# Loads of v for the first three chunks issued from GpSimd, and the first two scalings of k on VectorE, in a gated linear attention with a feed-forward layer behind it

## The chip, the core and the metric

The kernel runs on one core of a Trainium2 chip. The core has TensorE (matrix multiply, called PE in the profile, with its weight loads shown as PEld), VectorE (DVE), ScalarE (ACT), GpSimd (POOL) and SyncE (SP), which here does nothing but issue loads. The metric is the device time of one execution in microseconds (us); less is better. The kernel before has a median of 192.18 us over 11 runs.

## The reference

For each of 4 batches and 8 heads a state of 48 x 48 numbers is carried over 768 steps: it is decayed by alpha, row by row, and the outer product of k and v is added; the output is q times the state. The outputs of all heads are put side by side into rows of 384, and a feed-forward layer with a cosine gate follows:

```python
for t in range(S):
    state = alpha[:, :, t, :, None] * state + np.einsum('bhd,bhe->bhde', k[:, :, t], v[:, :, t])
    y[:, :, t] = np.einsum('bhd,bhde->bhe', q[:, :, t], state)
...
h = x @ w_in            # 3072 x 384 by 384 x 2048
g = h * np.cos(h)
return (g @ w_out).astype(np.float32)
```

## The kernel before

The 768 steps of a batch are cut into chunks of 128, so there are 24 chunks, each with all 8 heads: a tile has 128 rows (steps) and 8 x 48 columns. For a chunk the decay is turned into running sums of logarithms (ScalarE's logarithm in line 144, then a matmul with a triangle of ones in lines 157 and 161), and ScalarE takes the exponential of these and of their negatives (lines 177 and 175). k is multiplied by the one (`khat`, line 185) and q by the other (`qhat`, line 191), v is turned into bfloat16 (`vcast`, line 195), and a small tile `Em` holds the decay over the chunk (`emask`, line 200). TensorE transposes the scaled k and q (line 218), VectorE moves them out (line 224), TensorE forms the scores of each head (line 235), VectorE masks them (line 244), and TensorE forms the output from the scores and v (line 292) and from q and the state (line 289). The state is updated from k and v (line 260, then lines 272 and 274). The output is moved out (line 299), transposed (line 313) and moved out again (line 318), and goes through the feed-forward layer in two halves: matmul (line 330), cosine on ScalarE (line 338), gate on VectorE (line 344), matmul (line 352), eviction and store (lines 357 and 358).

Loads are of 192 KB. A chunk of k, q, v or alpha lies in memory as 8 heads of 128 rows of 48 floats, so each partition of the tile gets 8 runs of 192 bytes. `load` (lines 102 to 105) and `load_a` (line 100) issue them from SP, into pools of 6 tiles for each of k, q and v. The weights are four loads each of 768 KB (lines 111 and 124), cast by lines 115 and 117.

Nothing is scheduled by a planner. A string, `ORDER`, lists the steps by letter and chunk, and each engine does its share of them in that order; so each engine, and SP's queue of loads, works through a fixed list, and an instruction that waits holds up all that is behind it on its engine. `a0` loads alpha of chunk 0, `k0`, `q0`, `v0` the other inputs; `i0` is the logarithm of one chunk and `l1` that of chunks 2 and 3 together, `c0` and `C1` are the sums on TensorE, `d0` and `E1` the exponentials; `K0` is `khat`, `Q0` is `qhat`, `b0` is `vcast`, `E_0` is `emask`; `T0` are the transposes and `t0` their eviction, `A0` the scores, `m0` their masking, `Y0` the outputs, `y0` their eviction, `D0` the transposes of the output, `S0` and `u0` the state. `w19` are 19 matmuls on a tile of zeros (line 368), whose result is not used; there are 63 of these, all in the first part of the list. In what follows K0 and the like stand for these steps.

Before the first step of `ORDER`, VectorE clears some tiles and GpSimd builds two triangles of ones and an identity matrix. Of the scaling steps, Q0 and Q1 are on VectorE (`eng = nc.vector if j < 2 else nc.gpsimd` in `qhat`); all of K, all of b and all of E_ are on GpSimd.

Of the kernel before, what the change touches and what calls it, by code (L numbers as in the profile page):

```python
# [12 lines left out]
ALU = mybir.AluOpType  # L13
# [3 lines left out]
def kernel(  # L17
# [10 lines left out]
    nc = tc.nc  # L28
    B, H, S, D = q.shape
# [41 lines left out]
    khb, qhb = kqb[:, :, 0], kqb[:, :, 1]  # L71
# [16 lines left out]
    w2 = consts.tile([C, NF, DM], BF, tag="w2")  # L88

    a_t, q_t, k_t, v_t, cp_t, icp_t = {}, {}, {}, {}, {}, {}  # L90

    def rows(t, j):
        b, c = j // NC, j % NC
        return t[b, :, c * C : (c + 1) * C, :].rearrange("h s d -> s h d")
# [6 lines left out]

    def load(nm, src, d, j):
        t = inpool.tile([C, H, D], FP, tag=nm)
        nc.sync.dma_start(out=t, in_=rows(src, j))
        d[j] = t

    QF = DF // 4
# [74 lines left out]

    def khat(j):
        icp = icp_t[j // 2][:, j % 2]
        nc.gpsimd.tensor_tensor(out=khb[:, j % 3, :, 0:D], in0=k_t.pop(j),  # L185
                                in1=icp.rearrange("s (h d) -> s h d", h=H), op=ALU.mult)

    def qhat(j):
        cp = cp_t[j // 2][:, j % 2]
# [172 lines left out]
    def warmup(n):  # L362
# [8 lines left out]
    dve, act_e = nc.vector, nc.scalar  # L371
    units = {
        "a": load_a, "k": lambda j: load("k_sb", k, k_t, j), "q": lambda j: load("q_sb", q, q_t, j),
        "v": lambda j: load("v_sb", v, v_t, j), "z": load_w1, "Z": load_w2,
        "r": lambda h: cast_w1(h, dve, 0, 2), "s": lambda h: cast_w1(h, act_e, 2, 3), "R": cast_w2,

        "i": lambda j: ln(j, 1), "c": lambda j: cums(j, 1), "d": lambda j: exps(j, 1),
        "l": lambda g: ln(2 * g, 2), "C": lambda g: cums(2 * g, 2), "E": lambda g: exps(2 * g, 2),
        "K": khat, "Q": qhat, "b": vcast, "E_": emask,
        "T": transposes, "t": ev_transposes, "S": state, "u": ev_state,  # L380
        "A": scores, "m": mask_scores, "Y": outputs, "y": ev_outputs, "D": x_transposes, "B": ev_x,
# [4 lines left out]
    }  # L386

    ORDER = (
        "a0 i0 q0 c0 v0 a1 k0 k1 d0 Q0 E_0 i1 v1 K0 w19 T0 q1 t0 a2 b0 c1 d1 Q1 k2 v2 w2 A0 a3 K1 w3 T1 m0 t1 "
        "w6 A1 m1 a4 a5 Y0 b1 E_1 l1 y0 w7 D0 k3 B0 b2 q2 C1 E1 K2 q3 S0 u0 w3 Y1 Q2 Q3 y1 E_2 q4 w3 S1 u1 w3 "  # L390
        "D1 B1 w2 T2 t2 w4 A2 m2 l2 C2 w2 Y2 y2 K3 E2 k4 K4 w3 D2 B2 a6 a7 Q4 l3 w2 T3 t3 C3 w1 S2 u2 A3 m3 "
        "E3 v3 b3 w2 T4 t4 E_3 E_4 w5 A4 S3 z0 r0 s0 z1 z2 z3 r1 s1 F0 f_0 u3 m4 Y3 s2 F1 f_1 r2 y3 E_6 Z1 D3 "
# [23 lines left out]
    for u in ORDER.split():  # L416
        nm = u.rstrip("0123456789")
# [29 lines left out]
```

## Time and profile before

| | us |
|---|---|
| median of 11 runs | 192.18 |
| lowest and highest run | 191.54, 193.23 |
| the profiled execution's own time | 192.28 |
| its span in the profile | 190.5 |
| TensorE busy | 181.5 (95% of the span) |
| VectorE, ScalarE, GpSimd busy | 128.3, 119.1, 74.8 |

The span runs from the first to the last instruction that the profile records; 1.78 us of the execution's own time lie around it. Where the profile names what ended an idle time, it goes by the semaphore that came last. Instructions that only issue a transfer are not counted as busy time of an engine; the timeline shows them under SPq and ACTq, with the time that the issuing takes, and the landing is told apart from it: the 24 loads of v are issued from SP, with a median of 4.5 us from issue to landing. Of the bytes, 29.14 MB went over SP's queue and 4.72 MB over ScalarE's, which stores the output; there is no queue of GpSimd's among them. In the first 40th of the span (4.76 us) TensorE's row shows 0, in the others 9, up to the last with 2.

### The profile page before, as it was taken

The page shows a single profiled execution, that of the slowest core. Times are in us where ns is not written, and L with a number is a line of the kernel's source. Part 1 is how long each engine was busy: PE and PEld are TensorE (multiplying, and loading weights), DVE is VectorE, ACT ScalarE, POOL GpSimd, SP SyncE. Part 2 cuts the span into 40 slices and gives each one's busy share as a digit, 9 for nine tenths or more (in the row PEclk, how much of TensorE's full clock was granted, in tenths as well). Part 3 has the DMA queues.
Part 4 walks back from the last instruction along what each step waited for, and adds up shares of the span by engine and source line. Part 5 has one row for each costly group of instructions (what it writes and reads, how often), then busy time and mean ns, then how long its engine had stood idle before and what let it go on. Part 6 is the DMA issues. An engine that isn't in the chain of part 4 may idle for free.

```text
span 190.5 us, 5668 instructions
## 1 busy us (share of the span) xinstructions
PE 181.5 (95%) x2406; PEld 138.3 (73%) x2410; DVE 128.3 (67%) x159; ACT 119.1 (63%) x135; POOL 74.8 (39%) x116
## 2 busy tenths in 40 slices
PE   0999999999999999999999999999999999999992
PEld 0344545998766888697887688968769877797761
DVE  6128457999695489739667886895587685578520
ACT  3211447789555868985974989888596363364522
POOL 3422763212923451852971747155450475010000
PEclk9999999999999999999999999999999999999999
DMA  6999999999999999899999889997966899221112
GB/s 122 189 186 187 160 287 364 344 371 213 200 225 228 211 176 230 180 205 204 219 193 171 167 128 174 153 214 150 193 132 135 187 181 186 65 64 24 41 45 83
DMA packets 123225, 34.22 MB, mean 180 GB/s; under 512 B 116544, under 2 KB 121664, under 8 KB 123200
## 3 DMA queue, kind: packets, MB, share of 16 engines
q1 hardware_dynamic: 119744, 29.14, 82.1%
q10 hardware_dynamic: 3456, 4.72, 7.5%
q8 instruction: 19, 0.31, 0.7%
q14 instruction: 6, 0.05, 0.1%
HBM read 25.17 MB, written 4.72 MB: 157 GB/s over the span
## 4 chain that ended last, share of the span: by engine, by line
PE 88%; DMA 6%; POOL 2%; DVE 1%; ACT 1%; issue 1%; SPq 1%; DVEq 0%; ACTq 0%
PE t L330 33%; PE o_new L352 30%; PE w_new L368 8%; PE t L235 3%; PE t L218 3%; PE t L292 2%; DMA t<-kqb 2%; PE cum_new L157 2%; PE t L260 2%; PE t L289 2%; DMA t<-in_k_dram 2%; DMA a_new<-in_alpha_dram 2%; POOL kqb L185 2%; PE t L313 2%; PE cum_new L161 1%; DVE t L244 1%
## 5 line engine op out<-in xcount | busy, mean ns | idle before, releaser
L330 PE MATMUL t<-x,w 128*128 128x128 bf16 x1152 | 70.4, 219 | 0.0
L352 PE MATMUL o_new<-w,g_new 128*128 128x384 bf16 x384 | 68.8, 326 | 0.0
L344 DVE TENSOR_TENSOR g_new<-t,c_sb 128x1024 bf16<-128x1024 f32 x48 | 57.8, 1218 | 15.3 <-ACT c_sb L338 14.9
L330 PEld LDWEIGHTS <-w 128*128 128x128 bf16 x1152 | 65.6, 98 | 1.5
L338 ACT ACTIVATE c_sb<-t,halfpi 128x1024 bf16<-128x1024 f32 x48 | 52.3, 1112 | 18.5 <-PE t L330 15.6
L352 PEld LDWEIGHTS <-g_new 128*128 128x128 bf16 x384 | 35.4, 98 | 20.2
L244 DVE TENSOR_TENSOR t<-t,mask_f 128x1024 bf16<-128x1024 f32 x24 | 29.0, 1216 | 3.1 <-PE t L235 3.1
L185 POOL TENSOR_TENSOR kqb<-t,icp_new 128x384 bf16<-128x384 f32 x24 | 23.9, 1000 | 17.7 <-ACT icp_new L175 10.8
L274 POOL TENSOR_TENSOR ub<-sc,Em 128x384 bf16<-128x384 f32 x16 | 13.3, 829 | 39.6 <-DVE sc L272 39.6
L357 ACT ACTIVATE o_sb<-o_new 128x384 f32<-128x384 f32 x24 | 11.7, 488 | 26.0 <-PE o_new L352 26.0
L191 POOL TENSOR_TENSOR kqb<-t,cp_new 128x384 bf16<-128x384 f32 x22 | 22.0, 1008 | 12.0 <-DMA t<-in_q_dram 10.7
L299 DVE CAST t<-t 128x384 bf16<-128x384 f32 x24 | 13.3, 554 | 11.9 <-PE t L292 11.9
L175 ACT ACTIVATE icp_new<-cum_new 128x768 f32<-128x768 f32 (+1 forms) x13 | 9.8, 757 | 15.6 <-PE cum_new L161 15.1
L195 POOL CAST vpb<-t 128x384 bf16<-128x384 f32 x24 | 12.4, 518 | 18.1 <-DMA t<-in_v_dram 15.4
L368 PE MATMUL w_new<-warm 128*128 128x512 bf16 x63 | 19.0, 432 | 0.3 <-issue 0.2
L224 DVE COPY t<-t 128x1024 bf16<-128x1024 bf16 x13 | 8.9, 688 | 10.2 <-PE t L218 10.1
L144 ACT ACTIVATE lnab<-a_new 128x768 bf16<-128x768 f32 (+1 forms) x13 | 10.3, 794 | 5.4 <-DMA a_new<-in_alpha_dram 3.0
L137 ACT ACT_TABLE_LOAD x9 | 11.5, 1283 | 2.4 <-ACT o_sb L357 1.6
L338 ACT ACT_TABLE_LOAD x9 | 11.5, 1283 | 0.6 <-ACT o_sb L357 0.5
L272 DVE TENSOR_TENSOR sc<-t,ub 128x384 f32<-128x384 f32 x16 | 8.9, 554 | 4.5 <-PE t L260 4.4
L157 PE MATMUL cum_new<-lnab,triu_bf 128*128 128x384 bf16 x24 | 7.3, 333 | 4.5 <-ACT lnab L144 4.5
L292 PE MATMUL t<-vpb,t 128*128 128x48 bf16 x192 | 11.3, 183 | 0.2 <-DVE t L244 0.2
(43 smaller groups left out, 132.1 us busy)
## 6 DMA issues: line engine op xcount, KB each, us to landing
a_new<-in_alpha_dram SPq DMA_DIRECT2D x24, 192.0 KB, 4.6
t<-in_q_dram SPq DMA_DIRECT2D x24, 192.0 KB, 4.6
t<-in_v_dram SPq DMA_DIRECT2D x24, 192.0 KB, 4.5
t<-in_k_dram SPq DMA_DIRECT2D x24, 192.0 KB, 4.7
out_dram<-o_sb ACTq DMA_DIRECT2D x24, 192.0 KB, 3.3
w1f<-in_moe_w_in_dram SPq DMA_DIRECT2D x4, 768.0 KB, 7.5
w2f<-in_moe_w_out_dram SPq DMA_DIRECT2D x4, 768.0 KB, 10.9
t<-kqb SPq DMA_TRANSPOSE x11, 4.2
```

The lines of the kernel that those rows point to most:

```text
L185: nc.gpsimd.tensor_tensor(out=khb[:, j % 3, :, 0:D], in0=k_t.pop(j), in1=icp.rearrange("s (h d) -> s h d", h=H), op=ALU.mult)
L191: eng.tensor_tensor(out=qhb[:, j % 3, :, 0:D], in0=q_t.pop(j), in1=cp[:, 0:HD].rearrange("s (h d) -> s h d", h=H), op=ALU.mult)
L195: nc.gpsimd.tensor_copy(out=vpb[:, j % 3, :, 0:D], in_=v_t.pop(j))
L244: nc.vector.tensor_tensor(out=t.rearrange("s (h t) -> s h t", h=H), in0=A_ps.pop(j).rearrange("s (h t) -> s h t", h=H), in1=mask_f.unsquee ...
L274: eng.tensor_tensor(out=ub[:, us(j), :, 0:96].rearrange("r p (a e) -> r p a e", a=2), in0=sc.rearrange("r p (a e) -> r p a e", a=2), in1=E ...
L292: nc.tensor.matmul(t[:, h * D : (h + 1) * D], A_t[j][:, ACOL[h] * C : (ACOL[h] + 1) * C], vpb[:, j % 3, h], start=first, stop=True, skip_g ...
L299: nc.vector.tensor_copy(out=t, in_=y_ps.pop(j)[:, 0:HD])
L330: nc.tensor.matmul(t[:, f], w1[:, kk, ft * C : (ft + 1) * C], x_t[j][:, kk], start=(kk == 0), stop=(kk == 2))
L338: nc.scalar.activation(out=c_sb, in_=h_ps[j, half], func=AF.Sin, bias=halfpi, scale=1.0)
L344: nc.vector.tensor_tensor(out=g_new, in0=h_ps.pop((j, half)), in1=c_t.pop((j, half)), op=ALU.mult)
L352: nc.tensor.matmul(o_ps[j][:, 0:DM], g[:, f], w2[:, half * HF + f], start=(f == 0 and half == 0), stop=(f == HF - 1 and half == 1))
L368: nc.tensor.matmul(w_ps, warm[:, 0:C], warm, start=True, stop=True)
```

## The change

Three things are changed. The loads of v for chunks 0, 1 and 2 are issued by GpSimd instead of SP; a transfer issued from there has its descriptors made by software on GpSimd. In `ORDER` these three loads go to the front of the list, so that they are the first of its steps on GpSimd, behind the building of the constants; the loads left on SP keep their order. And K0 and K1 go from GpSimd to VectorE.

```diff
     def load(nm, src, d, j):
         t = inpool.tile([C, H, D], FP, tag=nm)
-        nc.sync.dma_start(out=t, in_=rows(src, j))
+        eng = nc.gpsimd if nm == "v_sb" and j < 3 else nc.sync
+        eng.dma_start(out=t, in_=rows(src, j))
         d[j] = t
...
     def khat(j):
         icp = icp_t[j // 2][:, j % 2]
-        nc.gpsimd.tensor_tensor(out=khb[:, j % 3, :, 0:D], in0=k_t.pop(j),
-                                in1=icp.rearrange("s (h d) -> s h d", h=H), op=ALU.mult)
+        eng = nc.vector if j < 2 else nc.gpsimd
+        eng.tensor_tensor(out=khb[:, j % 3, :, 0:D], in0=k_t.pop(j), in1=icp.rearrange("s (h d) -> s h d", h=H), op=ALU.mult)
...
     ORDER = (
-        "a0 i0 q0 c0 v0 a1 k0 k1 d0 Q0 E_0 i1 v1 K0 w19 T0 q1 t0 a2 b0 c1 d1 Q1 k2 v2 w2 A0 a3 K1 w3 T1 m0 t1 "
+        "v0 v1 v2 a0 i0 q0 c0 a1 k0 k1 d0 Q0 E_0 i1 K0 w19 T0 q1 t0 a2 b0 c1 d1 Q1 k2 w2 A0 a3 K1 w3 T1 m0 t1 "
         "w6 A1 m1 a4 a5 Y0 b1 E_1 l1 y0 w7 D0 k3 B0 b2 q2 C1 E1 K2 q3 S0 u0 w3 Y1 Q2 Q3 y1 E_2 q4 w3 S1 u1 w3 "
```

With this, VectorE's list begins, behind the clearing, with Q0, K0, t0, Q1, K1, m0, t1; GpSimd's, behind the constants, with the loads v0, v1, v2, then E_0, b0, b1, E_1, b2, K2; and SP's with the loads a0, q0, a1, k0, k1, q1, a2, k2, a3. Before, these were Q0, t0, Q1, m0, t1 on VectorE; E_0, K0, b0, K1, b1, E_1, b2, K2 on GpSimd; and a0, q0, v0, a1, k0, k1, v1, q1, a2, k2, v2, a3 on SP. TensorE's list is the same in both, all 63 matmuls on zeros included.

## Prediction

> **What bounds the kernel now.** I read the page's busy rows first, then TensorE's waits, then the timeline of the first 21 us, where the change lies.
>
> ```profile
> PE 181.5 (95%) x2406; PEld 138.3 (73%) x2410; DVE 128.3 (67%) x159; ACT 119.1 (63%) x135; POOL 74.8 (39%) x116
> ...
> DMA  6999999999999999899999889997966899221112
> ```
>
> TensorE is busy 181.5 of 190.5 us. Of the 9.0 us idle, 4.47 lie before its first matmul and 3.4 after its last (the final eviction starts at 187.14), so about 1.1 us is idle inside. The list of waits says the same; besides the first matmul's, no wait of TensorE is longer than 0.2 us:
>
> ```profile
> PE cum_new L157 <- ACT lnab L144: 4.5, 1, 4.5
> PE t L292 <- DVE t L244: 0.2, 1, 0.2
> PE t L218 <- POOL kqb L185: 0.2, 1, 0.2
> PE w_new L368 <- issue: 0.2, 1, 0.2
> ```
>
> So TensorE's own program, in its written order, sets the end. Part of it is filler: line 368's matmuls on a zero tile. The timeline (start, duration, engine, line, operation; in brackets the idle time before it and what ended that):
>
> ```profile
> 4.89 7.03 PE L368 MATMUL w_new<-warm 128*128 128x512 bf16 x19
> ...
> 6.02 0.57 POOL L200 TENSOR_TENSOR Em<-cp_new,m 128x8 f32<-128x8 f32 x1 [3.70 <-ACT cp_new L177]
> ...
> 6.99 0.52 ACT L144 ACTIVATE lnab<-a_new 128x384 bf16<-128x384 f32 x1 [1.05 <-DMA a_new<-in_alpha_dram]
> ...
> 8.07 0.99 POOL L185 TENSOR_TENSOR kqb<-t,icp_new 128x384 bf16<-128x384 f32 x1 [1.48 <-DMA t<-in_k_dram]
> ...
> 11.76 0.61 PE L218 MATMUL t<-ident_bf,kqb 128*128 128x128 bf16 x8
> ...
> 13.03 0.49 ACT L177 ACTIVATE cp_new<-cum_new 128x388 f32<-128x388 f32 x1
> ...
> 13.21 1.00 POOL L185 TENSOR_TENSOR kqb<-t,icp_new 128x384 bf16<-128x384 f32 x1 [3.70 <-ACT icp_new L175]
> ...
> 13.55 1.07 DVE L191 TENSOR_TENSOR kqb<-t,cp_new 128x384 bf16<-128x384 f32 x1 [0.46 <-ACT cp_new L177]
> ...
> 14.27 0.81 PE L218 MATMUL t<-ident_bf,kqb 128*128 128x128 bf16 x8 [0.18 <-POOL kqb L185]
> ...
> 15.48 0.84 ACT L144 ACTIVATE lnab<-a_new 128x768 bf16<-128x768 f32 x1 [1.96 <-DMA a_new<-in_alpha_dram]
> ```
>
> The first scaled k (K0) is done at 9.06, but TensorE's 19 filler matmuls run to 11.9 and stand ahead of the transposes T0 that use it. K0 has 2.7 us to spare already. That is the fact on which the forecast rests.
>
> **Part 1: K0 (k of chunk 0) from GpSimd to VectorE.** It costs 0.99 us on GpSimd; the like operation on VectorE, Q0, took 0.56 at 5.97 with a clear field. VectorE is idle from 6.53 to 12.40. K0 may end as late as 11.7 without moving T0. Worth: 0. The cover is the filler; with fewer filler matmuls K0 could be worth up to its 2.7 us, but the change keeps all 19.
>
> **Part 2: K1.** This one is not covered. Before, K1 ran on GpSimd (13.21 to 14.21) beside Q1 on VectorE, and TensorE's T1, whose filler ended at 14.07, waited 0.18 us for it. Now VectorE has Q1 and then K1, in that order; Q1 waits for the exponential that ends at 13.52, so K1, ready from 13.13, stands behind it. Q1 took 1.07 instead of 0.56 beside GpSimd's K1, so two such operations at once hold each other up. With a clear field both now take 0.47 to 0.56 each (the next instruction on VectorE starts some 0.09 before the last one's end): 13.55 + 0.47 + 0.56 = 14.58. T1's eight transposes then run in one piece, 0.45 us as T0's did in the chain: 15.07, against 15.08 before. The next two on VectorE, the masking m0 and the eviction t1, began at 14.55 and 15.68; they now begin at 14.49 and 15.62, and six fillers lie beside them. So with a clear field K1 is worth 0.0.
> The field is not clear: GpSimd's E_1 waits for the same exponential and its cast b2 comes next. A first row of that kind is above: Em at 6.02 took 0.57, not the 0.20 of its later run at 14.95, beside Q0. If E_1 gets between Q1 and K1 it costs 0.20; if a cast does as well, 0.50 more (L195's 0.50); if nothing does, the gain is the 0.06 above. Range -0.06 to +0.70; I take +0.20, since the row that it is nearest to is Em waiting behind Q0 and then going before the next. T1, then t1, then A1, all on TensorE's path, move by it, and nothing behind gives it back.
>
> **Part 3: three loads leave SP's queue.** SP issues one 192 KB load in 0.44 to about 1.0 us, and the loads land one by one: k0, the fifth, is used at 8.07, and the a3 load, the twelfth, ends a wait at 15.48. (15.48 - 8.07) / 7 = 1.06 us for each, 185 GB/s, with the DMA row at 9. The transfers, not the issues, are the limit here. The three v loads still move the same bytes, so the sum over the first twelve stays. What changes is the order. Bounds on a load's place: none of the v loads ahead of it, or all three.
>
> - k0: fourth to seventh, 6.99 to 10.2; K0 must start by 11.1. Covered by 0.9.
> - k1: fifth to eighth, 8.1 to 11.3; needed at 14.0.
> - q1: sixth to ninth, 9.1 to 12.3; needed at 13.55. Covered by 1.2.
> - a3: ninth to twelfth, at latest 15.48 as before. Its use on TensorE (C1) is at 18.77, behind the transposes of chunk 0's output, so an earlier a3 brings nothing.
>
> From the thirteenth load on the places are the old ones. Worth: 0.
>
> **Part 4: the issues on GpSimd.** They come after GpSimd's constants, whose last ends at 2.32, so v0 is issued later than before (1.85), not earlier. Behind them on GpSimd stand E_0, b0, b1, E_1, b2 and K2. First due is b0, for TensorE's Y0 at 16.74. No row of before shows an issue on GpSimd. Let g be what one takes of the engine. b0 is in time while 2.32 + 3g + 0.20 + 0.50 is below 16.74, that is while g is below 4.57 us. The rows for one load's issue, though on SP, are:
>
> ```profile
> L100 SPq DMA_DIRECT2D a_new<-in_alpha_dram x8: 444/996/2347, 0.7 to 20.3; - x8
> ...
> L104 SPq DMA_DIRECT2D t<-in_k_dram x7: 945/995/4022, 3.5 to 41.3; - x7
> ```
>
> Bounds 0.44 and 4.02, both without cost; I take 1.0, the median. The later ones of these also held the queue's backlog. Landing needs v0 by 16.2, and the median from issue to landing is 4.5. The moved K0 and K1 take 2.0 us off GpSimd up to 14.2, so the casts start earlier if the data is there. Worth: 0. If this cover is gone, each us of g above 4.57 costs 3 us.
>
> The Trainium skill, "DMA: Bandwidth & Descriptors", section "Anatomy of one DMA — SWDGE (gpsimd) path", gives some 2.0 us plus bytes / 436e3 for a DMA from GpSimd, an estimate of 2.45 us for 192 KB; three by that would be done at 9.7, and the sum would be the same 0. No run here shows it yet.
>
> A rule that speaks against the change stands in "SBUF — State Buffer" of the Trainium skill, section "Who interferes with whom": descriptors written by GpSimd stand still while VectorE runs a copy in a two-port mode. VectorE's first eviction copy here is t0 at 12.40, 0.69 us; an issue caught by it would be held by that much, and by the bound of 4.57 the sum stays 0. The same section says that two-operand VectorE work blocks only GpSimd work that reads SBUF; this case's 1.07 beside 0.56 for Q1 agrees.
>
> **Sum.** 0 + 0.20 + 0 + 0 = +0.2 us. The profiled execution took 192.28 (span 190.5 and 1.78 around it), which gives 192.48. It lay 0.1 above the median of the eleven runs, 192.18; against that median the forecast is 192.4. A measurement of this kernel can tell about 0.3%, 0.58 us, from no change, so the forecast counts as no change: 192.1 to 192.7 is its own range.
>
> **Rivals.**
>
> *Gaps close.* With GpSimd freer and loads earlier, TensorE's inner waits vanish: 0.2 + 0.2 + 0.2 from the list, 191.6. For: one of the three is T1's wait for K1 on GpSimd. Against: K1 is not earlier on VectorE, and the other two lie at 26.2 and 30.5, behind work that the change leaves alone. All 1.1 us inside would be 191.1, the floor.
>
> *Slow issue on GpSimd* (the slower side). One mechanism: making 1024 runs of 192 bytes into descriptors in software holds GpSimd for g each. It decides from g = 4.57, at Y0: 3 x (g - 4.57). At g = 5.2 that is +1.9, 194.1; at 6, +4.3, 196.5. For: SP's hardware takes 1.0 for it, and software may well take several times that. Against: it would have to be above the longest issue row, 4.02.
>
> *GpSimd gets in twice.* The casts wait for late v loads and fall between Q1 and K1: +0.70, or with a cast before Q1 as well +1.2; 192.9 to 193.4. For: 1.07 against 0.56 for Q1. Against: GpSimd has been free of K1 and should be through with b0 and b1 by 13.5.
>
> *Dearer transfers.* If a v load costs the DMA engines c instead of 1.06, q1 lands at 12.3 + 3(c - 1.06), past 13.55 from c = 1.48. At c = 2 that is +1.6, 193.8. For: another queue on the same engines. Against: same bytes, same runs.
>
> *Not what it says.* The v loads are not ahead of all of GpSimd's work (the constants are), and v0 is issued later; with b0 due at 16.74 that gives the forecast again, so it shares its chance.
>
> **How the numbers follow.** Forecast 0.50; gaps close 0.15; slow issue 0.13; getting in twice 0.14; dearer transfers 0.08. Faster by over 0.3% takes the gaps' 0.15 and 0.02 of the forecast; no change 0.47 of the forecast and 0.04 of getting in twice (up to +0.58); slower the rest, 0.32. The range: the low end is the 191.5 just under the gaps' price; the high end 194.1 takes in the two middle rivals and slow issue up to g = 5.2. Left out are the floor and larger g, some 0.1 to 0.2.
>
> **What would show it.** In the changed profile: T0 still at 11.8 behind 19 fillers (part 1); K1 on VectorE right after Q1, ending 14.6 to 14.8, T1 in one piece, A1 at 16.4 to 16.6 (part 2); the wait for a3's logarithm ending near 15.5 or earlier and C1 unmoved (part 3); E_0 on GpSimd starting near 5.5, b0 done long before 16.7 (part 4); a TensorE idle sum within 0.3 of before. Wrong it would be if T0 moves, if b0 ends after 16.7, if Q1 waits for q1's load, or if waits appear after 21 us, where I assume none.

## The result, and the profile after

The kernel after has a median of 194.90 us over 12 runs (194.02 to 197.83), the kernel before one of 192.07 over 47; the ratio is 1.014, with a 95% interval of 1.0118 to 1.0161. So the change made the kernel slower by 1.4%, some 2.7 us, where the forecast was no change (192.4) in a range up to 194.1. Ratios, here and below, leave disturbed runs out, so they aren't quite the quotients of the medians.

The profiled execution of after took 196.07 us, with a span of 194.2 and 1.87 around it: 1.2 above its median, so its 3.7 us over the span of before show the places of the loss rather than its exact size. Its page, rows in the order of the page (TensorE's busy time, the granted clock and the DMA share in 40 slices, then the chain that ended last):

```profile
PE 182.1 (94%) x2406; PEld 139.0 (72%) x2410; DVE 129.1 (66%) x161; ACT 119.1 (61%) x135; POOL 76.1 (39%) x117
...
PEclk9999999999999996999999999999999999999999
DMA  7999999998999989999799698999966798321112
...
PE 68%; DMA 14%; SPq 9%; DVE 3%; issue 2%; POOL 2%; ACT 2%; ACTq 0%; DVEq 0%; POOLq 0%
```

TensorE was busy 182.1 us, 0.6 more than before, in a longer span: the rest is idle time that was not there. In one slice, at 73 to 78 us, the granted clock is at 6 instead of 9. The chain, 88% TensorE before, now goes for 14% through DMA and for 9% through SP's issues. TensorE's waits name the places:

```profile
PE t L219 <- DVE sc L273: 1.9, 1, 1.9
PE t L219 <- DVE kqb L187: 1.0, 1, 1.0
PE t L293 <- DVE t L245: 0.2, 1, 0.2
PE t L331 <- DMA x<-t: 0.2, 1, 0.2
PE t L236 <- DMA t<-kqb: 0.2, 1, 0.2
```

The second line is T1's wait for K1, at 13.79, in the part that the prediction worked out. The first is new and lies far behind it. The front first, in the timeline (start, duration, engine, line, operation; in brackets the idle time before and what ended it):

```profile
2.27 2.81 POOL L105 DMA_DIRECT2D t<-in_v_dram  x3
...
4.84 5.83 PE L369 MATMUL w_new<-warm 128*128 128x512 bf16 x19
...
5.97 0.57 POOL L201 TENSOR_TENSOR Em<-cp_new,m 128x8 f32<-128x8 f32 x1 [0.89 <-ACT cp_new L178]
...
7.08 0.51 POOL L196 CAST vpb<-t 128x384 bf16<-128x384 f32 x1 [0.54 <-DMA t<-in_v_dram]
...
9.16 0.56 DVE L187 TENSOR_TENSOR kqb<-t,icp_new 128x384 bf16<-128x384 f32 x1 [2.68 <-DMA t<-in_k_dram]
...
10.50 0.61 PE L219 MATMUL t<-ident_bf,kqb 128*128 128x128 bf16 x8
...
12.36 0.59 DVE L192 TENSOR_TENSOR kqb<-t,cp_new 128x384 bf16<-128x384 f32 x1 [0.52 <-ACT cp_new L178]
12.49 0.83 POOL L196 CAST vpb<-t 128x384 bf16<-128x384 f32 x1
12.88 0.85 DVE L187 TENSOR_TENSOR kqb<-t,icp_new 128x384 bf16<-128x384 f32 x1
...
13.79 0.62 PE L219 MATMUL t<-ident_bf,kqb 128*128 128x128 bf16 x8 [0.96 <-DVE kqb L187]
...
15.45 0.84 ACT L145 ACTIVATE lnab<-a_new 128x768 bf16<-128x768 f32 x1 [3.19 <-DMA a_new<-in_alpha_dram]
```

GpSimd issued the three loads in 2.81 us, 0.94 each. K0 (line 187 at 9.16) was done at 9.72, before T0 at 10.50. K1 at 12.88 stood behind Q1 and took 0.85, beside a cast of GpSimd's of 0.83. The logarithm of a3 began at 15.45, against 15.48 before. Nothing was lost up to here: the first matmul of the feed-forward layer began at 32.43, against 33.20 before. That lead is not the change's, however: TensorE's 19 filler matmuls took 5.83 us instead of 7.03, and in the twelve profiles of the experiments, in whatever kernel, they took 5.48 to 6.30. The profile of before is the late one.

The loss begins at 53 us. If the start of each eviction of the output (line 358) is set against that of before, the first four are 0.8, 0.8, 0.5 and 0.3 us ahead, the fifth is 0.4 late, the sixth 2.6, the eighth 3.0, and the last ones 3.5. The timeline of ScalarE there:

```profile
53.15 0.49 ACT L358 ACTIVATE o_sb<-o_new 128x384 f32<-128x384 f32 x1 [1.32 <-PE o_new L353]
54.95 0.34 ACTq L359 DMA_DIRECT2D out_dram<-o_sb  x1
55.32 1.28 ACT L138 ACT_TABLE_LOAD   x1 [1.68 <-DMA a_new<-in_alpha_dram]
...
57.37 0.47 ACT L358 ACTIVATE o_sb<-o_new 128x384 f32<-128x384 f32 x1
59.31 0.34 ACTq L359 DMA_DIRECT2D out_dram<-o_sb  x1
59.75 0.84 ACT L145 ACTIVATE lnab<-a_new 128x768 bf16<-128x768 f32 x1 [1.91 <-DMA t<-in_v_dram]
...
61.89 0.49 ACT L358 ACTIVATE o_sb<-o_new 128x384 f32<-128x384 f32 x1
64.50 0.34 ACTq L359 DMA_DIRECT2D out_dram<-o_sb  x1
64.95 0.81 ACT L176 ACTIVATE icp_new<-cum_new 128x768 f32<-128x768 f32 x1 [2.57 <-DMA t<-in_v_dram]
```

ScalarE finished an output tile at 53.64 (53.15 + 0.49) and issued its store only at 54.95: 1.31 us in which it stood still, and the bracket of what comes behind says what ended it, a load of alpha. The next two stores were held 1.47 and 2.12 us, until loads of v had landed (59.31 - 57.84, 64.50 - 62.38). Before, each of the 24 stores was issued 0.03 us behind its tile. ScalarE works in order, so the exponential behind the store came at 64.95, against 63.13 before, and the cosines behind that. From there it goes over VectorE, which gates with the cosine, to TensorE; first VectorE's timeline, then TensorE's:

```profile
69.93 1.22 DVE L345 TENSOR_TENSOR g_new<-t,c_sb 128x1024 bf16<-128x1024 f32 x1 [2.41 <-ACT c_sb L339]
71.07 0.55 DVE L273 TENSOR_TENSOR sc<-t,ub 128x384 f32<-128x384 f32 x1
```

```profile
71.67 0.61 PE L219 MATMUL t<-ident_bf,kqb 128*128 128x128 bf16 x8 [1.93 <-DVE sc L273]
72.11 2.05 PE L331 MATMUL t<-x,w 128*128 128x128 bf16 x24
```

VectorE waited 2.41 us for the cosine, and its next operation (line 273, part of the state) ended at 71.62; TensorE, which has a transpose behind that, waited 1.93 us. Then the 24 matmuls of line 331 took 2.05 us instead of 1.50, in the slices where the granted clock is low (0.69 from 71 to 76 us). From these matmuls to the next transposes of line 219, the same work as before, it was 4.80 us (72.11 to 76.91) instead of 3.25. So a held store of 2 us became 1.9 us of idle TensorE and, at the lower clock, some 1.5 more. That second part belongs to this execution: its mean clock was 0.991, where ten of the twelve had 0.996 or more.

**Why stores wait for loads.** The built programs show it in their lists of instructions: every hardware transfer, SP's loads and ScalarE's stores in one count, takes the next of eight completion semaphores in turn, and the engine that issues it first waits until the transfer that had this semaphore last, eight back in the count, has landed. In the kernel before, stores 1 to 4 (counted from 0; written e1 to e4 in the expectations) come eight behind the loads k7, a9, v7 and q10. With three loads gone from SP's list, they come eight behind a8, v6, v9 and a13. In the trace of after, a8 is among four loads that SP issued from 50.06 on, and v6 among three from 54.52 on: loads that were just on their way. The Trainium skill, "DMA: Bandwidth & Descriptors", section "Anatomy of one DMA — SWDGE (gpsimd) path", says that transfers don't wait on semaphores themselves and that any such wait is served by the issuing engine ahead of it; the rows above agree, with 1.31 to 2.12 us of ScalarE.

### The profile page after: what moved, and what is told of

It reads as the page before. It is cut to its first block, busy times and chain, and to the rows that moved or that the text cites. A ratio compares the mean times of both kernels' runs of the same rounds, so it can differ in the third digit from the quotient of the medians.

```text
span 194.2 us, 5668 instructions
## 1 busy us (share of the span) xinstructions
PE 182.1 (94%) x2406; PEld 139.0 (72%) x2410; DVE 129.1 (66%) x161; ACT 119.1 (61%) x135; POOL 76.1 (39%) x117
## 3 DMA queue, kind: packets, MB, share of 16 engines
q1 hardware_dynamic: 116624, 28.55, 79.9%
## 4 chain that ended last, share of the span: by engine, by line
PE 68%; DMA 14%; SPq 9%; DVE 3%; issue 2%; POOL 2%; ACT 2%; ACTq 0%; DVEq 0%; POOLq 0%
PE t L331 26%; PE o_new L353 23%; DMA t<-in_q_dram 6%; SPq L105 5%; PE w_new L369 4%; DMA t<-in_k_dram 3%; PE t L236 3%; DMA t<-in_v_dram 2%; PE t L219 2%; SPq L100 2%; DMA x<-t 2%; PE t L293 2%; PE t L261 2%; PE cum_new L158 2%; PE t L290 1%
## 5 line engine op out<-in xcount | busy, mean ns | idle before, releaser
L353 PE MATMUL o_new<-w,g_new 128*128 128x384 bf16 x384 | 69.5, 328 | 0.0
L187 POOL TENSOR_TENSOR kqb<-t,icp_new 128x384 bf16<-128x384 f32 x22 | 22.0, 1000 | 16.3 <-ACT icp_new L176 8.5
L176 ACT ACTIVATE icp_new<-cum_new 128x768 f32<-128x768 f32 (+1 forms) x13 | 9.8, 757 | 16.7 <-PE cum_new L162 14.1
L369 PE MATMUL w_new<-warm 128*128 128x512 bf16 x63 | 17.8, 408 | 0.3 <-issue 0.2
```

The source lines that it names most:

```text
L187: eng.tensor_tensor(out=khb[:, j % 3, :, 0:D], in0=k_t.pop(j), in1=icp.rearrange("s (h d) -> s h d", h=H), op=ALU.mult)
L353: nc.tensor.matmul(o_ps[j][:, 0:DM], g[:, f], w2[:, half * HF + f], start=(f == 0 and half == 0), stop=(f == HF - 1 and half == 1))
L369: nc.tensor.matmul(w_ps, warm[:, 0:C], warm, start=True, stop=True)
```

## The experiments

The theory, called **pairs** here: the loss comes from which load each store has to wait for, and K on VectorE and the software issue are nearly free. Its rivals: **K1 on VectorE** costs more than the 0.2 us forecast; **software transfers** cost by themselves, through loads that come late. Each run was timed in five rounds beside the kernel before. The runs e1 to e4, e5 to e8, e9 to e11, and e12 were timed on four different chips, so runs of different groups are compared by their ratios.

| run | median, us | ratio to before, 95% interval | stores held over 0.1 us: number (us) |
|---|---|---|---|
| after | 194.90 | 1.0140, 1.0118 to 1.0161 | 1 to 4 (1.31, 1.47, 2.12, 1.15) |
| e1 K0, K1 alone | 192.93 | 1.0066, 1.0035 to 1.0097 | 5, 6 (1.16, 1.97) |
| e2 v alone | 194.45 | 1.0123, 1.0093 to 1.0154 | 0 to 4 (0.32, 1.01, 1.40, 1.94, 0.73) |
| e3 seven small loads | 195.30 | 1.0156, 1.0107 to 1.0204 | 5 to 7 (0.30, 1.07, 0.18) |
| e4 v from ScalarE | 193.86 | 1.0088, 1.0059 to 1.0117 | 1 to 5 (0.90, 1.34, 1.85, 0.88, 0.23) |
| e5 all, pairs restored | 194.13 | 1.0076, 1.0044 to 1.0107 | 7 to 9 (0.59, 0.15, 0.17) |
| e6 K alone, pairs restored | 193.17 | 1.0028, 0.9992 to 1.0064 | none |
| e7 v from ScalarE, pairs restored | 192.66 | 1.0016, 0.9985 to 1.0046 | 8 (0.13) |
| e8 small loads alone | 192.67 | 1.0016, 0.9990 to 1.0042 | none |
| e9 v alone, pairs restored | 193.63 | 1.0074, 1.0050 to 1.0097 | 7 to 9 (0.46, 0.41, 0.28) |
| e10 as e5, q1 ahead of k1 | 193.94 | 1.0059, 1.0034 to 1.0084 | 7, 9 (0.18, 0.35) |
| e11 as e5, v later | 194.19 | 1.0050, 1.0020 to 1.0081 | 7 (0.21) |
| e12 tiny loads from GpSimd | 192.32 | 0.9992, 0.9963 to 1.0020 | 7, 8 (0.48, 0.15) |

### e1 and e2: the two parts alone

e1 is the kernel before with the new `khat`; e2 is the kernel after with the old one:

```diff
 def khat(j):
-        eng = nc.vector if j < 2 else nc.gpsimd
-        eng.tensor_tensor(out=khb[:, j % 3, :, 0:D], in0=k_t.pop(j), ...)
+        nc.gpsimd.tensor_tensor(out=khb[:, j % 3, :, 0:D], in0=k_t.pop(j), ...)
```

> Only K0 and K1 go to VectorE; all loads of v stay on SP where they were. Each hardware transfer takes one of eight semaphores in turn and waits until the transfer that held it before has landed; in the built program the second to fifth output stores (e1 to e4), which ScalarE issues, wait here for the landing of k7, a9, v7 and q10, as in the kernel before. Theory A (the stores' semaphores: with three loads fewer on SP, e1 to e4 wait for a8, v6, v9 and a13 and hold ScalarE): 192.1 to 192.5 us, nothing beyond a few tenths at T1. Theory B (the software transfers of GpSimd crowd the first loads): 192.1 as before. Theory C (K1 behind Q1 on VectorE and the lock with GpSimd): the whole loss, about 194.9.

> Only the three loads of v go to GpSimd; K0 and K1 stay there too. The stores e1 to e4 wait for a8, v6, v9, a13, as in the changed kernel. Theory A (stores' semaphores): about 194.9 us, 194.2 to 195.5. Theory B (software transfers crowd the first loads): about 194.9 as well. Theory C (K1 on VectorE): 192.1.

Most of the loss, 1.0123 of 1.0140, is in the loads of v, and stores 1 to 4 are held as in after. But e1 is not free either, and its 192.93 lies in none of the three forecasts: it has stores 5 and 6 held, 1.16 and 1.97 us, with a wait of TensorE's of 1.8 us for VectorE behind them. Its program has those two stores eight behind the loads v10 and k16, where before they come behind the two stores ahead. So an edit that adds or takes away no transfer at all moved the pairs too.

### e3: seven small loads in a row, to bring the pairs back

```diff
+    def load_tiny(n):
+        nc.sync.dma_start(out=tiny[0:16, n], in_=q[0, 0, 16 * n : 16 * n + 16, :])
...
-        "... d1 Q1 k2 w2 A0 a3 K1 w3 T1 m0 t1 "
+        "... d1 Q1 k2 x0 x1 x2 x3 x4 x5 x6 w2 A0 a3 K1 w3 T1 m0 t1 "
```

The seven loads of 16 rows of 192 bytes are used by nothing; they only count.

> The changed kernel with all of its change, and seven loads of 3 KB on SP (16 rows of q into a tile that nobody reads) added behind the load of k2, which only take their turn of the eight semaphores: e1 to e4 then wait for q7, a9, v7, q10, nearly as in the kernel before (k7, a9, v7, q10). Theory A (stores' semaphores): the loss goes, 191.4 to 192.6 us. Theory B (software transfers): 194.9 or, with seven loads more, above. Theory C (K1 on VectorE): 194.9.

This failed as a test. Stores 1 to 4 were no longer held, but the seven issues in a row kept SP from 10.77 to 14.51 and the loads behind them came late: TensorE waited 0.6 us for the sums of chunks 2 and 3 and 0.6 us for T2, and the evictions were 1.2 us behind those of before from the first on, and 2.6 at the end. One loss was put in the place of the other, and 1.0156 says nothing about either.

### e4 and e7: the loads of v on ScalarE's queue

e4 takes software and K out of the question: the three loads leave SP, but ScalarE issues them, through hardware.

```diff
-        eng = nc.gpsimd if nm == "v_sb" and j < 3 else nc.sync
+        eng = nc.scalar if nm == "v_sb" and j < 3 else nc.sync
...
-        "v0 v1 v2 a0 i0 q0 c0 a1 k0 k1 d0 Q0 E_0 i1 K0 w19 ..."
+        "a0 i0 q0 c0 a1 k0 k1 d0 v0 Q0 E_0 i1 v1 v2 K0 w19 ..."
```

> The kernel before with the loads of v0, v1 and v2 issued by ScalarE's hardware queue in its idle time behind the first exponentials; no GpSimd transfer, K0 and K1 on GpSimd. As many hardware transfers as before, but SP's list is three loads shorter, and e1 to e4 are paired with a8, v6, v9, a13, exactly as in the changed kernel. Theory A (stores' semaphores): about 194.9 us, 194.0 to 195.6, though nothing of the change is in it. Theory B (software transfers): 192.1. Theory C (K1 on VectorE): 192.1.

e7 is e4 with seven small loads, one each behind a2, k2, a3, a4, a5, k3 and q2, so that SP is nowhere held for long:

```diff
-        "... w19 T0 q1 t0 a2 b0 c1 d1 Q1 k2 w2 A0 a3 K1 w3 T1 m0 t1 "
+        "... w19 T0 q1 t0 a2 x0 b0 c1 d1 Q1 k2 x1 w2 A0 a3 x2 K1 w3 T1 m0 t1 "
```

> Run e4 (v0 to v2 from ScalarE's hardware queue, K on GpSimd; 193.86) with seven loads of 3 KB on SP, one behind each of a2, k2, a3, a4, a5, k3, q2, which pair e0 to e6 as in the kernel before. Theory A: 191.6 to 192.6. If instead issuing these loads from ScalarE, or their place among the first loads, is what e4 paid for: still about 193.9.

e4 loses 0.9% without any software transfer and without K on VectorE; e7 loses nothing that can be measured, and the intervals, 1.0059 to 1.0117 and 0.9985 to 1.0046, lie apart. e4's 193.86 lies 0.14 us under the pairs theory's range and far above the 192.1 of the two others; e7's 192.66 lies 0.06 above its range. This pair shows the theory. ScalarE's timeline of e4, and then of e7, at the third of the stores:

```profile
57.37 0.49 ACT L358 ACTIVATE o_sb<-o_new 128x384 f32<-128x384 f32 x1
59.20 0.34 ACTq L359 DMA_DIRECT2D out_dram<-o_sb  x1
59.64 0.84 ACT L145 ACTIVATE lnab<-a_new 128x768 bf16<-128x768 f32 x1 [1.78 <-DMA t<-in_v_dram]
```

```profile
57.63 0.49 ACT L363 ACTIVATE o_sb<-o_new 128x384 f32<-128x384 f32 x1 [0.36 <-PE o_new L358]
58.16 0.39 ACTq L364 DMA_DIRECT2D out_dram<-o_sb  x1
58.78 0.84 ACT L150 ACTIVATE lnab<-a_new 128x768 bf16<-128x768 f32 x1 [0.65 <-DMA a_new<-in_alpha_dram]
```

In e4 the store stands 1.34 us behind its tile (59.20 - 57.86), and a load of v ends the idle time; in e7 it comes 0.04 us behind.

### e5, e6 and e8: the pairs restored in after and in e1

e5 is the kernel after with eight small loads spread as in e7 (the eighth behind q3), which gives all the stores their old partners; e6 is e1 with one; e8 is the kernel before with the eight, as the control for what they cost.

```diff
-        "... w19 T0 q1 t0 a2 b0 c1 d1 Q1 k2 w2 A0 a3 K1 w3 T1 m0 t1 "
+        "... w19 T0 q1 t0 a2 x0 b0 c1 d1 Q1 k2 x1 w2 A0 a3 x2 K1 w3 T1 m0 t1 "
```

> The changed kernel whole (v0 to v2 from GpSimd, K0 and K1 on VectorE), with eight loads of 3 KB on SP, one behind each of a2, k2, a3, a4, a5, k3, q2, q3, into a tile that nobody reads. In the built program every one of the stores e0 to e6 then waits for the same load as in the kernel before (e1: k7, e2: a9, e3: v7, e4: q10), where the changed kernel has a8, v6, v9, a13. Run e3 had nearly these pairs but its seven loads stood in a row and held SP for 3.7 us, so that C1 and T2 came late. Theory A (the stores' waits hold ScalarE): no store held, 191.6 to 192.9 us. Theory B (the software transfers crowd the first loads): still about 194.9.

> Run e1 (K0 and K1 on VectorE only; 192.93) with one load of 3 KB on SP behind a2. The built program then pairs e5 with e4 and e6 with e5, as in the kernel before, where e1 had v10 and k16; nothing else is different. Theory A: e1 lost its time at the stores e5 and e6, held 1.2 and 2.0 us in its profile; without that 191.8 to 192.4. Theory C (K1 behind Q1, T1 waiting for it): still about 192.9.

> The kernel before with the same eight loads of 3 KB on SP as e5 and nothing else: what the small loads cost by themselves. The stores e1 to e4 wait for earlier loads than before (k6, v5, a11, q8). Theory A: 191.9 to 192.7, as no store can be held by these; were the small loads themselves costly, above that, and e5 and e7 would have to be read against it.

With the old pairs the loss of after falls from 1.0140 to 1.0076, and these two intervals lie apart as well. But e5's 194.13 lies between the two forecasts, 192.9 at most and about 194.9, and meets neither. K alone falls from 1.0066 to 1.0028, with an interval that contains no loss; it overlaps that of e1, and e6's 193.17 is nearer to the 192.9 of theory C than to 192.4, so this pair settles nothing. The small loads cost 0.16%, or nothing. So the held stores are about half of the loss of after, 0.6% (some 1.2 us). The other half, 0.76% less what the small loads take, was still there, and it is not K: TensorE's waits of e5 offer two places.

```profile
PE t L224 <- DVE kqb L192: 1.0, 1, 1.0
PE t L336 <- DVE w L123: 0.9, 1, 0.9
```

One is T1 behind K1, which stands behind Q1, which waited until 12.65 for q1's load; the other is the first weights, landing late at 33 us. The profile can't say what they cost: e5's profiled execution took 193.0, 1.1 us under its median, and its evictions come within 0.05 us of those of e8, from the first (49.81 and 49.76) to the last (187.62 and 187.57).

### e9, e10, e11: what is left

e9 is e2 with eight small loads; e10 is e5 with q1 ahead of k1 on SP; e11 is e5 with the three loads still on GpSimd, but at the places that e4 has for them.

```diff
 e10
-        "v0 v1 v2 a0 i0 q0 c0 a1 k0 k1 d0 Q0 E_0 i1 K0 w19 T0 q1 t0 a2 ..."
+        "v0 v1 v2 a0 i0 q0 c0 a1 k0 q1 k1 d0 Q0 E_0 i1 K0 w19 T0 t0 a2 ..."
 e11
+        "a0 i0 q0 c0 a1 k0 k1 d0 v0 Q0 E_0 i1 v1 v2 K0 w19 T0 q1 t0 a2 ..."
```

> The three loads of v from GpSimd in the changed order, K0 and K1 left on GpSimd, and the same eight small loads of 8 lines of 48... rows that give the stores their old partners. Pairs theory: no store of e1 to e4 is held over 0.2 us, against 0.3 to 1.9 us in the run of the v loads alone. About what was left of 1.0076 in the run with everything and the pairs restored: if K1 on VectorE behind a late q1 is the cause (a wait of 1.0 us at T1), this kernel has no wait over 0.3 us there, and gives 1.001 to 1.004, as the small loads alone did (1.0016). If the software loads cost later loads their time on the DMA engines, and so the weights at 33 us, that is all still here: 1.006 to 1.009, with a wait for the weights near 33 us.

> The changed kernel with the eight small loads, and SP's load of q1 moved ahead of that of k1. If the late q1 is the cause of what was left, Q1 on VectorE starts when its exponential is done (near 12.4 instead of 12.65) and T1's wait of 1.0 falls to 0.7 or less, unless k1 is now the one that is late; the ratio falls to 1.003 to 1.006. If the software loads cost later loads their time, nothing changes: 1.007 to 1.009. No hold of e1 to e4 in either.

> The changed kernel with the eight small loads, and the three loads of v issued from GpSimd not ahead of its other work but later: v0 before the mask of chunk 0, v1 and v2 behind it. If it is the place of the software loads ahead of k0, k1 and q1 that costs (q1 late, T1 waits 1.0), they now come behind these: T1 waits 0.3 to 0.6 and the ratio is 1.002 to 1.005. If the software loads cost by their being so made, wherever they stand: 1.007 to 1.009, with weights late near 33 us. No hold of e1 to e4 in either.

e9 has K on GpSimd and no wait at T1 over 0.2 us, and still loses 0.74%. So K1 behind a late q1 is not what was left; the three loads on GpSimd's queue are. The interval, 1.0050 to 1.0097, lies apart from that of e8 (the small loads alone) and from that of e7, which has the same loads off SP but in hardware. Against e2, 1.0123, it is a third pair for the stores, though these two intervals just touch. A rival is in the table: e9 has stores 7 to 9 held, with their old partners. In its profile that moved nothing, since the evictions behind them come within 0.1 us of those of e8, which has none held (store 10: 109.50 and 109.44), and e12, with 0.48 and 0.15 us held, lost nothing.

e10 and e11 came out at the upper edge of what was expected of a late q1 (1.0059 and 1.0050), and their intervals reach into both expectations, so they settle nothing on the place of these loads; T1's wait in e10 was 0.8, not the 0.7 or less that was expected. What they show is where an earlier front goes. TensorE's waits of e11:

```profile
PE t L336 <- DVE w L123: 1.0, 1, 1.0
PE t L336 <- DMA x<-t: 1.0, 1, 1.0
PE t L241 <- DMA t<-kqb: 0.4, 1, 0.4
PE t L224 <- DVE kqb L192: 0.3, 1, 0.3
```

T1's wait fell from 1.0 to 0.3, and the wait for the weights took it up, 1.0 where e5 had 0.9. The second line is a place of loss that neither theory covers, at 162 us: late in the kernel 22 transposes are not TensorE's but transfers that SP issues, and one of them landed late. Such a wait stands in the profiles of six of the seven kernels with K on VectorE (after 0.2, e1 0.4, e3 0.7, e6 0.9, e10 0.2, e11 1.0; e5 has none) and in none of the seven with K on GpSimd. Why is open, and one profile of each kernel may mislead.

### e12: GpSimd issues, but hardly any bytes

The kernel before, with three loads more of 16 rows of 192 bytes, issued by GpSimd ahead of all else.

```diff
+        nc.gpsimd.dma_start(out=tiny[0:16, n], in_=moe_w_in[16 * n : 16 * n + 16, 0:D])
...
-        "a0 i0 q0 c0 v0 a1 ..."
+        "x0 x1 x2 a0 i0 q0 c0 v0 a1 ..."
```

> The kernel before, with three tiny loads more (16 rows of 192 bytes each, used by nothing) that GpSimd issues ahead of its other work; all loads of v stay on SP, K0 and K1 stay on GpSimd, the stores keep their old partners. With the pairs restored, the three loads of v from GpSimd cost 1.0074 where the same from ScalarE cost 1.0016 and the small loads alone 1.0016. If that half per cent belongs to GpSimd's having issued transfers at all (its software, the time around the span, which was 2.0 us instead of 1.8 there), it shows here: 1.004 to 1.008. If it belongs to the 0.59 MB that went that way, among the other early loads and SP's issues of 2 us beside them, this kernel is within 0.999 to 1.003, SP's issues of q1 and a2 take about 1 us as before, and the first casts of the weights do not wait longer than before. In neither is a store of e1 to e4 held over 0.2 us.

The stores have their old partners here too, as in e5 to e7 and e9 to e11. No loss, with an interval that lies apart from e9's. So it is not that GpSimd issues transfers at all (0.55 us a load here), but something in the size of these: the 0.59 MB, or the 1024 runs of each. One thing it does is seen in SP's timeline: the issues of q1 and a2 in e9, then in e7 (the same loads off SP, in hardware), then in e12:

```profile
4.54 2.00 SPq L105 DMA_DIRECT2D t<-in_q_dram  x1
6.58 2.05 SPq L100 DMA_DIRECT2D a_new<-in_alpha_dram  x1
```

```profile
4.88 0.71 SPq L105 DMA_DIRECT2D t<-in_q_dram  x1
5.64 0.98 SPq L100 DMA_DIRECT2D a_new<-in_alpha_dram  x1
```

```profile
6.82 0.88 SPq L104 DMA_DIRECT2D t<-in_q_dram  x1
7.74 1.04 SPq L100 DMA_DIRECT2D a_new<-in_alpha_dram  x1
```

While the software transfers run, an issue on SP takes twice as long. That is no mark of software, though: in e4, beside the loads from ScalarE, the issues of k2, a3 and a5 took 1.73, 1.96 and 2.04 us. That the half per cent comes of this is not shown: the profiled spans of e7 and e9, 191.0 and 191.2 us, hardly differ where the medians differ by 1.0, so the profile of e9 doesn't hold the loss. A quarter of it may lie around the span, which takes 2.03 us in the median of e9's runs (1.96 in e2's), against 1.78 in e7's; but in after, e10 and e11, whose K is on VectorE, it is 1.77 to 1.81, so the software loads alone don't make it, and in e12, which lost nothing, it is 1.95. Where the rest goes stays open.

## Why the prediction failed, step by step

**Part 1 (K0) was right.** K0 on VectorE took 0.56 us, as the row of Q0 said, and was done 0.78 us before T0, under the cover of the filler. It is worth 0. The cover was thinner than forecast: T0 came at 10.50 and not at 11.8, as the fillers ran faster than in the profile that the working went by.

**Part 2 (K1) came out at its size by luck.** K1 stood behind Q1 and T1 ran in one piece, as forecast. From the end of the filler to the end of T1 it was 3.16 us before and 3.34 in e1, e3 and e6: 0.18, where 0.20 was taken. But the 0.20 stood for E_1 getting between Q1 and K1, and it didn't. In e1 (E_1 is line 200, Q1 191, K1 186):

```profile
12.06 0.56 DVE L191 TENSOR_TENSOR kqb<-t,cp_new 128x384 bf16<-128x384 f32 x1 [0.46 <-ACT cp_new L177]
12.11 0.57 POOL L200 TENSOR_TENSOR Em<-cp_new,m 128x8 f32<-128x8 f32 x1 [1.42 <-ACT cp_new L177]
12.54 0.56 DVE L186 TENSOR_TENSOR kqb<-t,icp_new 128x384 bf16<-128x384 f32 x1
...
13.15 0.62 PE L218 MATMUL t<-ident_bf,kqb 128*128 128x128 bf16 x8 [0.55 <-DVE kqb L186]
```

E_1 ran beside Q1, and Q1 and K1 took what they take in the clear field, for which the working came to 0.0. The 0.18 is T1 instead: counted with 0.45 us from the end of K1, it took 0.05 to start and then 0.62. In after the sum was 3.74, +0.58, inside the range up to 0.70: K1 took 0.85 beside a cast. The reading that two such operations hold each other up was half right: before, Q1 took 1.07 for 0.56, but GpSimd's K1 beside it 1.00, and K0 alone 0.99. "Nothing behind gives it back" was too strict, since e11's wait for the weights took an earlier T1 up again.

**Part 3 (three loads leave SP's queue) is the step that failed.** It held as far as it was worked out: in after Q1 waited for its exponential and not for q1, and a3's logarithm began at 15.45 (in e5 Q1 did wait for q1, until 12.65: its exponential was due about 12.0 there, not at 13.55, since the fillers ended at 10.33 instead of 11.92). What failed is its last line, "From the thirteenth load on the places are the old ones. Worth: 0." The places in SP's order are the old ones. The place in the count of all hardware transfers, loads and stores together, is not, and on that count it hangs which load a store waits for. By after against e5 that is worth about 0.6%, 1.2 us. Its second half failed as well: "the three v loads still move the same bytes, so the sum over the first twelve stays" takes a software transfer for a hardware one, and e9 against e8 puts 0.6%, 1.1 us, on the difference, whose mechanism stays open. Added up they make 1.2 of the 1.4% by which after is slower; the rest is within the intervals, and so is K by itself (e6).

**Part 4 (the issues on GpSimd) was right.** One issue took 0.94 us, where 1.0 was taken, and b0 was done at 7.59, far before 16.7. The estimate by the skill's formula, 2.45 us for a load, is not what the trace shows: the median from issue to landing was 5.8 us, for three in a row. It decided nothing. All three were issued by 5.08, ahead of VectorE's first eviction copy, so no run here shows whether such a copy holds an issue up.

**The rivals.** *Slow issue on GpSimd* did not happen (0.94 against 4.57). *GpSimd gets in twice* happened in part, beside K1 instead of between: 0.58 of its 0.70. *Dearer transfers* came nearest, in its sign and its sender, but not in its mechanism: the profile has the three loads at 1.6% of 16 engines' time, 194.2 x 0.016 / 3 = 1.04 us each, no more than the 1.06 of a load from SP, and q1 did not come past 13.55.

```profile
q1 hardware_dynamic: 116624, 28.55, 79.9%
...
q0 software_dynamic: 192, 0.59, 1.6%
```

*Gaps close* was wrong. The prediction's own last paragraph named the sign that would refute it, "if waits appear after 21 us, where I assume none"; they appeared, from 54 us on. No view of the profile of before shows a store that is about to be held, since none was: it could only have been read by following, in the built programs, which transfer each store waits for.

## What to carry to other kernels

A load that is added, removed or sent over another queue also changes what later transfers wait for, if completion semaphores are handed out in turn: compare the waits of every transfer in the two programs, above all of those that a computing engine issues, before calling an edit at one end of the kernel local. When a change is late far from where it was made, look first for an engine that stands still between finishing a tile and issuing its store. And a transfer moved to GpSimd has to be measured as another kind of transfer, not as the same bytes from elsewhere.

## What the runs showed of the hardware that was not expected

- The software queue moved 0.59 MB in 192 packets, 3 KB each, where SP's queue has 116624 packets for 28.55 MB, 245 bytes each. The engines' time per load is the same all the same (1.04 and 1.06 us).
- In after, the issues of q1, a2 and k2 on SP, behind the software loads of 192 KB, took 1.98 to 2.05 us, where in before they took 0.97 to 1.15; three tiny software loads left them at 0.88 to 1.04. Three hardware loads from ScalarE lengthened some of SP's issues as much (e4: 1.73 to 2.04).
- The same 19 filler matmuls took 7.03 us in one profile and 5.48 to 6.30 in all the others. They start 0.43 us apart at first and then 0.21, and the step comes at 10.4 us in before, at 7.8 in after. "TensorE: Matmul & The Clock Gate" of the Trainium skill, section "Part 1: The HAM clock gate (the "warmup" mystery)", says that the clock's window runs free, so the slow start differs from run to run; these rows agree, and a gain of under 1 us at the front of a single profile means little for this reason.
- After 1.93 us without work TensorE's granted clock fell, to 0.69 in the mean from 71 to 76 us, and 24 matmuls took 2.05 us instead of 1.50. In e4 and e2, which waited 1.4 and 1.6 us at the same place, the mean clock of the run stayed at 1.000, and in e1, with a wait of 1.8 us until 90.69, at 0.998.
